# Part of a seven-tap convolution moved from VectorE to GpSimd, and VectorE's calls in another order

## The chip, the cores and the metric

The kernel runs on one core of a Trainium2 chip. The core has TensorE (PE in the profile; its weight loads are PEld), VectorE (DVE), ScalarE (ACT), GpSimd (POOL) and SyncE (SP, which here only issues DMAs). Each engine works through its own list of instructions in order, and the engines wait for one another with semaphores. The metric is the device time of one execution in microseconds (us), as the median of several runs; less is better.

## The reference

The input x has 8 sequences of 4096 tokens with 192 channels. A causal convolution with seven taps runs along the tokens; its weights are a softmax over the taps, one set for each of 8 heads of 24 channels. Its result goes through a feed-forward layer with the exact GELU. The output has 32768 rows of 192.

```python
w = softmax(weight)                                   # 8 heads x 7 taps
x_pad = concatenate([zeros(B, 6, D), x], axis=1)
conv = einsum('hk,bskhg->bshg', w, unfold(x_pad, 7))  # (32768, 192)
h = conv @ w_in                                       # (32768, 2048)
g = 0.5 * h * (1 + erf(h / sqrt(2)))
out = g @ w_out                                       # (32768, 192)
```

## The kernel before

**Tiling.** The tokens are cut into two halves, and both halves are worked side by side: partitions 0 to 63 hold channels of one half, partitions 64 to 127 those of the other. A *block* n takes w tokens from each half, 256 in blocks 0 to 5 and 512 in blocks 6 to 34, so there are 35 blocks. The 192 channels are three *parts* of 64.

**Stages of a block.** SP loads x into one of three buffers `xin`. VectorE transposes it into `xT` (function `trans`, called t below; two buffers). GpSimd copies the last six tokens of the block before into the front of `xT` (`halo`). Then the taps: tap k multiplies a shifted `xT` by a weight for each partition and adds it to `acc` (two buffers). From block 9 on ScalarE makes the first tap, k=0, in three instructions of one part each (`first_tap`). VectorE makes taps 1 to 6 (`conv`, called c1 to c6 below), each one instruction over 1536 elements a partition; c6 writes the bf16 tile `xc`. TensorE makes the first product in 16 *slots* (`mm1`): slot i is 12 matmuls into one of two PSUM buffers `hp`, and ScalarE applies GELU to it and writes it to `gT`. Slot i+2 needs the GELU of slot i, as its buffer is the same. After the 12 matmuls of each slot TensorE makes a share of the second product of the block before (block n-1), in groups of four matmuls, *rounds* below.

**Two kinds of blocks.** Odd blocks from 9 to 33 (the list `ST`, type "S") make their second product by a scheme with fewer matmuls, 44 rounds and not 48. It needs sums of GELU results: VectorE makes `S1`, `S3`, `Dn` and `S4` in pieces (`st_add`; "S1_0" is the first piece of S1), two DMAs from GpSimd's queue with an addition make more (`st_dma`), and the pieces of the result are put together afterwards: ScalarE copies parts out of PSUM (`st_copy`: p5, p1, e, u, p3, -u, -g) and VectorE adds them (`st_post`: k0, k3, k4). All other blocks are type "N". VectorE transposes every block's result from PSUM or SBUF into `osb` (`evac_t`, `st_evac`, three pieces ev0 to ev2), and SP stores it. PSUM's four 512-wide banks of `ob` go from one block's second product to the next; `release` names the instruction that frees a bank.

**The order of the work.** It is written out by hand. TensorE works on block n while VectorE convolves block n+1 or n+2. VectorE's list is a sequence of *loops*, one for the convolution of each block. `plan` has a loop's own calls: t of the next block and then c1 to c6. `AT_ST` and `at_ev` place the other calls: (2, 1, 0, "S1", 0) means the loop of the block's number plus 2, ahead of that loop's call 1. ScalarE's list has 16 GELUs for each block, and `AT_COPY` and `TAPS` say ahead of which slot's GELU a copy or a first tap goes. `ROUNDS` says how many rounds of a type S block's second product follow each slot. GpSimd's list has, for each n, `halo(n)` and then the DMAs of block n-2. SP's list alternates `load(n+4)` and `store(n-1)`.

In the steady state an even block on TensorE carries the second product of a type S block, and an odd block that of a type N block.

Of the kernel before, what the change touches and what calls it, by code (L numbers as in the profile page):

```python
# [11 lines left out]
def bass_lightweight_conv__then__act_gelu_exact_kernel(  # L12
# [16 lines left out]
    TB = 512  # L29
# [42 lines left out]
    ST = [m for m in range(M0 + 3, M1) if m % 2 == 1]  # L72
    K0 = {n: i for i, n in enumerate([4, 5, 6, *range(9, NB)])}
# [48 lines left out]
    with es:  # L122
# [61 lines left out]
        S_K0 = sem("S_K0")  # L184
        S_WT = sem("S_WT")
# [55 lines left out]
        def wait_pc(e, n, p):  # L241
# [11 lines left out]
            n: [(0, 0, 2), (0, 2, 1)] * (n not in K0) + [(k, 0, NP) for k in range(1, KS)]  # L253
            for n in range(NB)
            if n not in PC
        }
        FQ = F // 8
# [55 lines left out]
        def wait_banks(t, m, g):  # L313
# [5 lines left out]
            elif g % 2:  # L319
                t.wait_ge(S_GELU, SL0[NB] - 1 + g // 2)  # L320
            else:
                for b in LAST[g : g + 2]:
                    t.wait_ge(*release(OWNER[b], b))
# [96 lines left out]
        for e, (at, hf, cg, u, k) in enumerate(EVENTS):  # L420
            FIRST.setdefault((UNIT[u][0], cg), e)
        DONE.discard(len(EVENTS) - 1)
        DONE = sorted(DONE)
        ROUNDS = (3, 3, 2, 3, 3, 2, 3, 3, 2, 4, 3, 3, 2, 3, 3, 2)
        assert sum(ROUNDS) == 44

        def st_done(e, m, name):
# [5 lines left out]
        COPIES = ("p5", "p1", "e", "u", "p3", "-u", "-g")  # L433
        AT_COPY = {
            "p5": (1, 6), "p1": (1, 8), "e": (1, 14), "u": (2, 0), "p3": (2, 2), "-u": (2, 6), "-g": (2, 10),
        }

        def ac(m, name):

            return len(COPIES) * ST.index(m) + COPIES.index(name) + 1  # L440

        POSTS = ("k0", "k3", "k4")

        def dp(m, name):

            return len(POSTS) * ST.index(m) + POSTS.index(name) + 1

        SUMS = {"S1": (0, 4, 6, 8), "S3": (6, 8), "Dn": (0, 4, 8), "S4": (0, 4, 8)}

        def sa(m, name, k):  # L450
# [3 lines left out]
        AT_ST = [  # L454
            (2, 1, 0, "S1", 0), (2, 1, 2, "Dn", 0), (2, 1, 4, "S4", 0), (2, 1, 6, "S1", 1),
            (2, 2, 2, "S1", 2), (2, 2, 4, "S3", 0), (2, 3, 0, "Dn", 1), (2, 4, 0, "S4", 1),
            (2, 5, 0, "k0", 0), (3, 1, 0, "ev", 2),
            (3, 6, 0, "k3", 0), (4, 1, 1, "ev", 1), (4, 1, 5, "k4", 0), (4, 2, 0, "ev", 0),
        ]

        def at_ev(n):

            if n == M0:
                return [(3, 1, 3), (3, 2, 1), (3, 2, 3)]
            return [(3, 1, 3), (3, 2, 1), (3, 2, 3)]
# [3 lines left out]
        for n in range(M0, M1):  # L469
            if n not in ST:  # L470
                SIDE += [((n + at[0], *at[1:]), "ev", n, j) for j, at in enumerate(at_ev(n))]
            else:
                SIDE += [((n + d, o, r), name, n, q) for d, o, r, name, q in AT_ST]
        SIDE.sort(key=lambda q: q[0])
        EV = {}
        for _, name, n, j in SIDE:
            if name in ("ev", "evac"):
                EV[n, j] = EVC[M0 - 1] + len(EV) + 1

# [833 lines left out]
```

## Time and profile before

| What | Value |
|---|---|
| median of 3 runs | 669.4 us (668.56 to 669.79) |
| profiled execution, its own time | 667.87 us |
| its span, first to last instruction | 666.1 us |
| granted TensorE clock | 1.00 |
| busy: TensorE, ScalarE, VectorE, GpSimd | 661.4, 610.8, 600.7, 47.6 us |
| GELU: 510 instructions, mean | 1022 ns |
| a tap of 1536 elements on VectorE: mean | 1811 ns |
| t (transposition of a 512 token block): mean | 2369 ns |
| first tap, one part on ScalarE: mean | 718 ns |

The busy time of an engine is what its instructions cover; the ends of TensorE's matmuls are modelled, so its busy share alone doesn't say that it runs at its peak. The profile's parts used below are: the busy table, the chain of work that ended last, the busy times in chosen windows, and the timeline of one engine, whose lines have the start, the length, the engine, the line of the kernel, the tiles and, in brackets, the idle time before and what ended it.

### The profile page before, as it was taken

Reading aid. Unit: us, or ns where it says so; the run is one execution under the profiler, and the core shown is the slowest. Engines: PE = TensorE matmul, PEld = TensorE weight load, DVE = VectorE, ACT = ScalarE, POOL = GpSimd, SP = SyncE. Lnnn points to the kernel's source line nnn. Section 1 sums busy time; section 2 is a strip of 40 time slices with the busy share of each in tenths; the row PEclk is TensorE's granted clock in tenths of the full one; section 3 lists DMA queues with packets and bytes.
Section 4 is the critical chain, followed back from the end, with each engine's and each line's share of the span. In section 5 each row is a group of like instructions: output and inputs, shape, how many; then the busy total and the mean of one; then the engine's idle time right before and its main releaser. Section 6 shows DMA issues by size and latency. Waiting matters only on the chain.

```text
span 666.1 us, 27567 instructions
## 1 busy us (share of the span) xinstructions
PE 661.4 (99%) x12712; PEld 516.4 (78%) x12712; DVE 600.7 (90%) x510; ACT 610.8 (92%) x720; POOL 47.6 (7%) x87
## 2 busy tenths in 40 slices
PE   8999999999999999999999999999999999999998
PEld 8999655557667787877878778787787878878787
DVE  6979999799999999999999999999999999999632
ACT  8999988889999999999999999999999999999884
POOL 7000000010000100001010010100001000010100
PEclk9999999999999999999999999999999999999999
DMA  9735334243081461905529073370824719151233
GB/s 159 165 89 130 65 69 97 72 93 79 18 197 29 107 135 34 203 7 127 114 41 201 3 163 78 62 179 2 191 50 91 151 29 192 22 118 29 56 90 97
DMA packets 137028, 63.92 MB, mean 96 GB/s; under 512 B 126800, under 2 KB 133520, under 8 KB 136912
## 3 DMA queue, kind: packets, MB, share of 16 engines
q1 hardware_dynamic: 129136, 49.37, 33.2%
q0 software_dynamic: 6656, 12.19, 10.1%
q8 instruction: 100, 1.64, 1.1%
q10 hardware_dynamic: 1120, 0.59, 0.3%
q14 instruction: 16, 0.13, 0.1%
HBM read 28.31 MB, written 25.17 MB: 80 GB/s over the span
## 4 chain that ended last, share of the span: by engine, by line
PE 99%; ACT 0%; DVE 0%; DMA 0%; issue 0%; ACTq 0%
PE hp L1066 50%; PE ob L1150 23%; PE ob L1202 18%; PE ob L1106 5%; PE ob L1258 1%; PE hp L1258 1%; PE ob L1011 0%; DMA wsb<-in_weight_dram 0%; PE ob L1066 0%; ACT dg L912 0%; DVE wcol L772 0%; ACT xc L237 0%; ACT osb L347 0%; ACT wex L899 0%; ACT xTb L269 0%
## 5 line engine op out<-in xcount | busy, mean ns | idle before, releaser
L974 ACT ACTIVATE gT<-hp 128x1024 bf16<-128x1024 f32 x510 | 513.0, 1022 | 43.0 <-PE hp L1066 35.7
L1066 PE MATMUL hp<-xc,win 64*64 64x512 bf16 (+2 forms) x6036 | 438.4, 366 | 0.2
L1066 PEld LDWEIGHTS hp<-xc,win 64*64 64x64 bf16 (+1 forms) x6036 | 247.2, 106 | 73.0 <-ACT gT L974 4.6
L827 DVE SCALAR_TENSOR_TENSOR acc<-xT,wcol,acc 128x1536 f32<-128x1536 f32 (+1 forms) x165 | 282.9, 1714 | 10.6 <-ACT acc L938 7.3
L1150 PE MATMUL ob<-gT,wot 64*64 64x512 bf16 x2880 | 205.6, 376 | 0.0
L1202 PE MATMUL ob<-gT,wot 64*64 64x512 bf16 x832 | 158.0, 376 | 0.0
L1150 PEld LDWEIGHTS ob<-gT,wot 64*64 64x64 bf16 x2880 | 112.1, 107 | 43.3
L1202 PE MATMUL ob<-gT,wst 64*64 64x512 bf16 (+2 forms) x832 | 144.0, 323 | 0.0
L1202 PE MATMUL ob<-s_S,wot 64*64 64x128 bf16 (+2 forms) x624 | 89.9, 305 | 0.0
L800 DVE STREAM_TRANSPOSE xT<-xin 128x1536 f32<-128x1536 f32 (+2 forms) x39 | 76.2, 1963 | 3.8 <-DMA xin<-in_x_dram 1.4
L1202 PEld LDWEIGHTS ob<-gT,wst 64*64 64x64 bf16 x832 | 68.5, 107 | 10.7
L1202 PEld LDWEIGHTS ob<-gT,wot 64*64 64x64 bf16 x832 | 63.9, 107 | 1.5
L938 ACT ACTIVATE acc<-xT,wcol 128x512 f32<-128x512 f32 (+1 forms) x87 | 61.2, 703 | 0.0
L827 DVE SCALAR_TENSOR_TENSOR xc<-xT,wcol,acc 128x1536 bf16<-128x1536 f32 (+1 forms) x33 | 56.7, 1720 | 0.8
L1202 PE MATMUL ob<-s_S,wst 64*64 64x512 bf16 x208 | 57.4, 376 | 0.0
L1202 PE MATMUL ob<-s_Dn,wst 64*64 64x512 bf16 x208 | 57.4, 376 | 0.0
L1202 PEld LDWEIGHTS ob<-s_S,wot 64*64 64x64 bf16 x624 | 50.2, 107 | 8.6
L545 POOL DMA_DIRECT2D gT<-gT x26 | 22.4, 861 | 318.1 <-DVE s_S L559 318.1
L1106 PE MATMUL ob<-wout,gT 64*128 64x192 bf16 x768 | 41.9, 243 | 0.0
L1106 PEld LDWEIGHTS ob<-wout,gT 64*128 64x128 bf16 x768 | 35.1, 94 | 3.3
L373 DVE STREAM_TRANSPOSE osb<-ob 128x512 f32<-128x512 f32 x45 | 31.1, 694 | 6.2 <-PE ob L1150 6.2
L559 DVE TENSOR_TENSOR s_S<-gT 128x1024 bf16<-128x1024 bf16 (+1 forms) x39 | 32.6, 837 | 1.4 <-ACT gT L974 1.3
(78 smaller groups left out, 322.6 us busy)
## 6 DMA issues: line engine op xcount, KB each, us to landing
out_dram<-osb SPq DMA_DIRECT2D x124, 192.0 KB, 3.6
xin<-in_x_dram SPq DMA_DIRECT2D x116, 192.0 KB, 4.2
gT<-gT POOLq DMA_DIRECT2D x13, 512.0 KB, 4.6
gT<-gT POOLq DMA_DIRECT2D x13, 256.0 KB, 3.3
xin<-in_x_dram SPq DMA_DIRECT2D x18, 96.0 KB, 2.5
wout<-in_moe_w_out_dram POOLq DMA_DIRECT2D x4, 192.0 KB, 4.7
win<-in_moe_w_in_dram POOLq DMA_DIRECT2D x4, 96.0 KB, 4.3
win<-in_moe_w_in_dram POOLq DMA_DIRECT2D x2, 192.0 KB, 4.5
```

What stands on the lines that cost most here:

```text
L373: v.transpose(osb_t(m, j), bank(BK[m][j])).then_inc(S_EV)
L545: e.dma_start(quad(m, 1, 0, k, k1 - k), quad(m, 0, 0, k, k1 - k), accum_op=ALU.add).then_inc(S_AD[q], 16)
L559: ins = v.tensor_tensor(t("S1"), quad(m, 1, 0, k, n), quad(m, 1, 1, k, n), ALU.add)
L800: v.transpose(out, src).then_inc(S_TR)
L827: ins = v.scalar_tensor_tensor(dst, src, wk, a, op0=ALU.mult, op1=ALU.add)
L938: a.activation(out=acc[n % 2][:, p * TB : p * TB + w], in_=ap(xT[n % 2], p * XW + HX, [[NP * XW, 128], [1, w]]), func=AF.Copy, scale=wcol[ ...
L974: a.activation(out=ap(gT[n % 2], (i % 2 * NF + i // 2) * TB if n in ST else i * c * 2 * w, dst), in_=ap(ob, 2 * TB, [[4 * TB, 128], *src[1 ...
L1066: ins = t.matmul(hbuf(u, slice(fo, fo + fw), o, w), ap(win, f1, [[NP * F, 64], [2, fw]]), xc[n % 2][r, p * TB : p * TB + w], start=(p == 0 ...
L1106: ins = t.matmul(bb[sub], gT[m % 2][r, c0 : c0 + 128], wout[r, CH[sub][i] * C : (CH[sub][i] + 1) * C], start=(ph == 0 and k == 0), stop=(p ...
L1150: ins = t.matmul(bank(BK[m][j], slice(64 * h, 64 * h + 64), w), ap(wot, 64 * hf * NF * C + CH[h][i] * C + 64 * j, [[NF * C, 64], [1, 64]]) ...
L1202: ins = t.matmul(bank(BK[m][bk], slice(64 * cg, 64 * cg + 64))[:, c0 : c0 + w], wt_, x, start=(e == mine[0]), stop=(e == mine[-1] or e in ...
L1258: ins = t.matmul(banks(m, g)[h], gT[m % 2][:, c0 : c0 + 128], wout[:, CH[h][i] * C : (CH[h][i] + 1) * C], start=(i == 0), stop=(i == NF - 1),)
```

## The change

The change does four things.

1. From block 11 on (block 10 keeps seven whole taps) one tap of each block is split. VectorE makes only part 2 of it (512 elements). GpSimd makes parts 0 and 1 in two instructions (`tap_g`): the product of `xT` and the weight is written into the block's `xin` buffer, which the transposition has emptied, and a second instruction adds it to `acc`. In odd blocks this is tap 2, in even blocks tap 4 (`GT`). GpSimd waits for VectorE's tap before it; VectorE's next tap waits for GpSimd's addition (`S_GT`), and so does the load that refills `xin`.
2. VectorE's calls are in another order. In even loops: ev2, c1, c2, k3, c3, k4, ev1, t, S1_0, the third of tap 4 (g), Dn_0, c5, ev0, S1_1, c6. In odd loops: S4_0, ev0 and ev1 of a type N block, S1_2, S3, c1, t, ev2, Dn_1, g, S4_1, k0, c3, c4, c5, c6. Before, t came first in each loop.
3. ScalarE's copies and first taps are ahead of other slots. In an even block: first taps at slots 5, 11, 12 (before 2, 4, 10), p5 at 7 (6), p1 at 9 (8), e at 14 as before. In an odd block: p3 at 1 (2), u at 2 (0), -u at 3 (6), -g at 5 (10), first taps at 8, 10, 13 (4, 8, 12).
4. `ROUNDS` has 4 and 1 rounds after slots 13 and 15 (before 3 and 2). A bank's two halves are freed separately. The tile `tq` has a second buffer, `wtf`. `st_add` has a wait that only two type S blocks in a row would use; there are none here.

TensorE's matmuls are the same in number and shape.

```diff
+    TYPE = {m: "S" if m in ST else "N" for m in range(-4, NB + 4)}
+    LOOPS = {'NNS': 't123456', 'NSN': '1tg3456', 'NSS': '1tg3456', 'SNS': '123tg56', 'SSN': '1tg3456'}
+    FIRST_AT = {'NSN': (5, 11, 12), 'NSS': (4, 8, 12), 'SNS': (8, 10, 13), 'SSN': (12,)}
...
+    ORDER = {n: LOOPS.get(kind(n), "t123456") if n > M0 + 3 else "t123456" for n in range(M0 + 3, NB)}
+    GT = {n: next(k for k in range(1, KS) if str(k) not in o) for n, o in ORDER.items() if "g" in o}
+    PG = 2
...
+        def tap_g(e, n):
+
+            w, kt = WS[n], KS - 1 - GT[n]
+            src = ap(xT[n % 2], HF + kt, [[NP * XW, 128], [XW, PG], [1, w]])
+            z = ap(xin[n % NX], 0, [[TB // 32 * DQ, 128], [TB, PG], [1, w]])
+            a = ap(acc[n % 2], 0, [[NP * TB, 128], [TB, PG], [1, w]])
+            e.tensor_scalar(z, src, wcol[:, kt : kt + 1], None, ALU.mult).then_inc(S_GT)
+            e.wait_ge(S_GT, 2 * list(GT).index(n) + 1)
+            e.tensor_tensor(a, a, z, ALU.add).then_inc(S_GT)
...
-        ROUNDS = (3, 3, 2, 3, 3, 2, 3, 3, 2, 4, 3, 3, 2, 3, 3, 2)
+        ROUNDS = (3, 3, 2, 3, 3, 2, 3, 3, 2, 4, 3, 3, 2, 4, 3, 1)
...
-        AT_COPY = {
-            "p5": (1, 6), "p1": (1, 8), "e": (1, 14), "u": (2, 0), "p3": (2, 2), "-u": (2, 6), "-g": (2, 10),
-        }
+        AT_COPY = {'NN': {'p5': (1, 7), 'p1': (1, 9), 'e': (1, 14), 'p3': (2, 1), 'u': (2, 2), '-u': (2, 3), '-g': (2, 5)}}
...
-        AT_ST = [
-            (2, 1, 0, "S1", 0), (2, 1, 2, "Dn", 0), (2, 1, 4, "S4", 0), (2, 1, 6, "S1", 1),
-            (2, 2, 2, "S1", 2), (2, 2, 4, "S3", 0), (2, 3, 0, "Dn", 1), (2, 4, 0, "S4", 1),
-            (2, 5, 0, "k0", 0), (3, 1, 0, "ev", 2),
-            (3, 6, 0, "k3", 0), (4, 1, 1, "ev", 1), (4, 1, 5, "k4", 0), (4, 2, 0, "ev", 0),
-        ]
+        AT_ST = {'NN': [(1, 4, 10, 'S1', 0),
+                (1, 5, 9, 'Dn', 0),
+                (1, 6, 12, 'S1', 1),
+                (2, 0, 3, 'S1', 2),
+                (2, 0, 6, 'S3', 0),
+                (2, 0, -3, 'S4', 0),
+                (2, 2, 8, 'Dn', 1),
+                (2, 3, 6, 'S4', 1),
+                (2, 3, 7, 'k0', 0),
+                (3, 0, 5, 'ev', 2),
+                (3, 2, 4, 'k3', 0),
+                (3, 3, 9, 'ev', 1),
+                (3, 3, -3, 'k4', 0),
+                (3, 6, 1, 'ev', 0)]}
+        AT_EV = {'NS': [(3, 0, -2), (3, 0, 3), (3, 2, -3)], 'SS': [(3, 0, -2), (3, 0, 3), (3, 2, -3)]}
...
+            if n - NX in GT:
+                e.wait_ge(S_GT, 2 * list(GT).index(n - NX) + 2)
...
-            for n in range(3, M1 + 2):
+            for n in range(3, M1 + 3):
                 if n < NB:
                     halo(n)
+                if n - 1 in GT:
+                    g.wait_ge(S_HALO, n)
+                    g.wait_ge(S_CV, cvd(n - 2) + [q[0] for q in CALLS[n - 1]].index(GT[n - 1]))
+                    tap_g(g, n - 1)
...
+                if n in GT and k == GT[n] + 1:
+                    v.wait_ge(S_GT, 2 * list(GT).index(n) + 2)
```

## The prediction

> **What bounds the kernel now.** I read the page's busy table and the chain of work that ended last first.
>
> ```profile
> PE 661.4 (99%) x12712; PEld 516.4 (78%) x12712; DVE 600.7 (90%) x510; ACT 610.8 (92%) x720; POOL 47.6 (7%) x87
> ...
> PE 99%; ACT 0%; DVE 0%; DMA 0%; issue 0%; ACTq 0%
> ```
>
> TensorE is the chain from end to end. Since its matmul ends are modelled, that alone doesn't show that it runs at its peak, so I asked for the busy times of single pairs of blocks (one odd, one even), among them the last, where VectorE has far less to do.
>
> ```profile
> 278.88:319.48 40.60, 40.60 (x791) 32.66 (x786) 39.20 (x32) 38.45 (x46) 2.46 (x4) 1.00 0.47 98
> 563.12:603.73 40.61, 40.61 (x794) 32.66 (x787) 39.18 (x32) 38.46 (x46) 2.55 (x4) 1.00 0.40 87
> 603.73:644.34 40.61, 40.61 (x793) 32.79 (x787) 28.22 (x26) 36.08 (x41) 1.71 (x2) 1.00 0.28 61
> ```
>
> The columns after the stretch and its length are the busy times of PE, PEld, DVE, ACT and POOL. VectorE falls from 39.2 to 28.2 us and the pair still takes 40.61: TensorE sets the pace, and VectorE's freed time buys nothing. Next, TensorE's own timeline, in which any late operand would show as an uneven step.
>
> ```profile
> 246.25 0.87 PE L1066 MATMUL hp<-xc,win 64*64 64x512 bf16 x12
> 246.90 0.87 PE L1150 MATMUL ob<-gT,wot 64*64 64x512 bf16 x12
> ...
> 276.90 0.41 PEld L1066 LDWEIGHTS hp<-xc,win 64*64 64x64 bf16 x12 [0.21 <-ACT gT L974]
> ...
> 276.91 0.89 PE L1066 MATMUL hp<-xc,win 64*64 64x512 bf16 x12
> ```
>
> Twelve matmuls take 0.65 us, so a round of four takes 0.216, and a slot with three rounds 1.295. The steps are even to a few hundredths. The one place where ScalarE nearly delays TensorE is slot 8 of an even block (last two lines): the GELU of slot 6 ends at 276.84, the weight loads start 0.05 later, the matmuls just in time; that block loses 0.02 us. So the question is not what VectorE gains, but which engine now comes late for TensorE. ScalarE is the nearest.
>
> ```profile
> 247.50 2.00 ACT L974 ACTIVATE gT<-hp 128x1024 bf16<-128x1024 f32 x2
> 249.52 0.59 ACT L598 ACTIVATE tq<-ob 64x512 f32<-64x512 f32 x1
> 250.14 1.95 ACT L974 ACTIVATE gT<-hp 128x1024 bf16<-128x1024 f32 x2
> 251.99 0.71 ACT L938 ACTIVATE acc<-xT,wcol 128x512 f32<-128x512 f32 x1
> 252.60 1.01 ACT L974 ACTIVATE gT<-hp 128x1024 bf16<-128x1024 f32 x1
> 253.87 1.02 ACT L974 ACTIVATE gT<-hp 128x1024 bf16<-128x1024 f32 x1 [0.26 <-PE hp L1066]
> 254.92 0.63 ACT L598 ACTIVATE uu<-uu 64x512 f32<-64x512 f32 x1
> 255.57 1.94 ACT L974 ACTIVATE gT<-hp 128x1024 bf16<-128x1024 f32 x2
> ```
>
> From start to start: GELU to GELU 0.92; GELU to a first tap (L938) 0.92, and 0.61 from there to the next GELU; to p3 (or p5) 1.05 and 0.62; to -u (or -g) 1.05 and 0.65; to u (or p1) 0.92 and 0.48. A slot is 1.295, so a GELU with a copy (1.56 to 1.70) runs 0.3 to 0.4 late and the next slot gives 0.37 back. Before, the extras stand at least two slots apart. A GELU can start 0.92 after its slot's first matmul (253.87 against 252.95 for slot 5).
>
> **The change, part by part.** Times in an odd block count from its first matmul (246.25 above).
>
> *VectorE's work.* 24 taps (blocks 11 to 34) shrink from 1536 to 512 elements. The profile has 1.81 us for 1536 and 1.02 for 768, so 512 take about 0.75: 24 x 1.06 = 25 us less busy, worth 0 by the windows above; only ScalarE's schedule and the new waits are left.
>
> *ScalarE's copies in odd blocks.* p3, u, -u stand at slots 1, 2, 3, -g at 5. GELU 0 starts at 0.97 (kept back by that of the slot before), p3 2.02, GELU 1 2.64, u 3.56, GELU 2 4.04, -u 5.08, GELU 3 5.74, which ends at 6.76. Slot 5 is due at 4 x 1.295 + 0.65 + 4 x 0.216 = 6.69 and can start about 0.08 after that end: **0.15 us lost**. Then GELU 4 6.66, -g 7.71, GELU 5 8.36, ending 9.38; slot 7, due at 9.28 + 0.15, loses 0.03. Together 0.18 in each of 12 odd blocks (11 to 33): 2.2 us. If p3, -u and -g cost only 0.92 ahead of them, this is 0; if starts slip by 0.1, 0.3.
>
> *The first tap at slot 8 and t.* Odd block o's slot 8 makes the first tap of block o+2, which needs t of that block; t now stands behind k3, c3, k4 and ev1 in VectorE's list. k3 waits for -u and k4 for -g.
>
> ```profile
> 255.58 0.69 DVE L608 TENSOR_TENSOR tq<-tq,uu 128x512 f32<-128x512 f32 x1 [0.96 <-ACT uu L598]
> 256.19 1.81 DVE L827 SCALAR_TENSOR_TENSOR xc<-xT,wcol,acc 128x1536 bf16<-128x1536 f32 x1
> 258.09 2.41 DVE L800 STREAM_TRANSPOSE xT<-xin 128x1536 f32<-128x1536 f32 x1
> ```
>
> These lines show the links: k3 0.03 after -u ends, the next call 0.61 later, a tap 1.81, t 2.40. -u ends at 5.71: k3 5.74, c3 6.35 to 8.16, k4 after -g (8.34) at 8.37, ev1 8.97, t 9.60 to 12.00. The tap would start at 11.3 and starts at 12.06 (0.06, as GpSimd's copy follows VectorE below), GELU 8 at 12.67, ending 13.69. Slot 10, due at 10 x 1.295 + 2 x 0.216 (two slots have four rounds) + 0.18 = 13.56, can start at 13.77: **0.21 lost** in 11 odd blocks (11 to 31): 2.3 us. This is one to one in t's end: at 11.8 it is 0, at 12.3 0.5.
>
> *Even blocks.* Slots with 3, 3, 2 rounds: GELU 4 5.89, first tap 6.81, GELU 5 7.42, GELU 6 8.33, p5 9.38, GELU 7 10.00, ending 11.02; slot 9, due at 9 x 0.65 + 24 x 0.216 = 11.03, loses 0.07, and the 0.02 of slot 8 goes: 0.05 in 13 blocks, 0.65. The first taps at 11 and 12 end with GELU 12 at 17.6, slot 14 due at 17.73. ROUNDS moves one round from slot 15 to slot 13: nothing in the sum.
>
> *GpSimd's pair.* Its product has one input: 256 elements took 0.405, 18 took 0.210, so 1024 about 1.04 (at most 1.10, by the 768-element copy of 0.822). The addition has two: 256 bf16 elements took 0.614. Bounds for 1024: 1.24 with the slope of one input, 2.46 in proportion; I take 1.86, the row's slope over the smallest copy's 0.2. With 0.06 between them: 3.0 (2.3 to 3.6). In the even loop it starts at 8.22, behind c3, and ends at 11.2 (at the latest 11.85), while VectorE runs k4, ev1 and t.
>
> ```profile
> 242.22 0.20 POOL L723 COPY xT<-xT 128x18 f32<-128x18 f32 x1 [14.88 <-DVE xc L827]
> ...
> 267.10 0.96 POOL L723 COPY xT<-xT 128x18 f32<-128x18 f32 x1
> ```
>
> The same copy takes 0.20 next to t and 0.96 when it starts inside a tap (266.20 to 268.00); it ends 0.06 after the tap. So GpSimd waits for a VectorE instruction that reads two SBUF tiles, and the reverse is likely. Next is S1_0, which reads two, at 11.94: no meeting, 0. In the odd loop the pair starts behind c1; t and ev2 cover 2.9 us, and Dn_1 may wait up to 0.75. That loop's c6 ends 1.3 us before TensorE needs `xc`: hidden; without that cover, 12 x 0.75 = 9 us. The next tap, g's successor c3 or c5, comes 3 us or more after the pair.
>
> [...]
>
> *Other moved calls.* ev0 of a type N block frees the bank for the first rounds of an even block: S1_0 11.94, g 13.05, Dn_0 13.7, c5 14.85, ev0 16.6, S1_1 17.2, c6 17.8, S4_0 19.5, that ev0 20.6 to 21.35, needed at 20.72 + 0.39 + 0.65 = 21.76: margin 0.3 with the weight load ahead. Then t ends 6.45 into the even block, its tap is due at 6.8. p5, p1 and k0 come 0.6, 0.8 and 2 us before TensorE reads them. VectorE now idles some 2.7 us a pair at k3. On SP, `load` waits for the pair, and the stores behind it need ev calls of a later loop anyway; x is there over 30 us before t. On POOL, the DMA for S1_0 is queued behind the pair, but S1_0 itself comes later than its end; `halo` waits only for c6. All cost 0.
>
> *Sum.* 2.2 + 2.3 + 0.65 = 5.1 us on the profiled execution's 667.87 (span 666.1, 1.8 around it): 673.0. That execution is 1.5 under the median of 669.4, so I forecast **674.5**.
>
> **The rivals.** *No change.* The three losses are each 0.05 to 0.2 us, against rows known to 0.02 to 0.05; if TensorE starts a little closer behind a GELU and t ends 0.2 sooner, all vanish: 669.4. *k4 counts as a two-input instruction.* It reads PSUM and SBUF; if it waited for GpSimd's product (until 9.3), t and the tap at slot 8 would come 0.95 later: 11 x 0.95 = 10 more, 685. No row has such a pair. *GpSimd is half as fast as taken.* A pair of 5.8 ends at 14.0 and holds S1_0 by 2.1, of which 0.3 is margin: 1.8 x 11 = 20 more, 694. It decides from a pair of 4.1 us on; the rows stop at 3.6. *Faster.* The pitch of a round (0.216 us) would have to shrink because VectorE touches SBUF less: 1% of some 465 us (186 to 652) would be 4.5 us, 665. It counts from 0.3% of the pitch on; the last pair, with VectorE down to 28 us and the same 40.61, speaks against it.
>
> **How the numbers follow.** Forecast (1.5 to 9 us more) 0.60, no change 0.18, k4 0.09, GpSimd slow 0.08, faster 0.05. 0.2% (1.3 us) is about what a measurement tells here. Slower 0.77, the same 0.18, faster 0.05. The range from 669.0 to 685.5 leaves out the fast case, a little of no change and the slow GpSimd.
>
> **What would show it.** Pairs of 41.0 us; idle TensorE or weight loads ended by GELUs at slots 5 and 10 of odd blocks; about 0.7 us of ScalarE's idle time before its first tap, ended by t; k3 waiting some 2.7 us for -u; VectorE 25 us less busy; GpSimd's addition near 1.9 us. Wrong if pairs stay 40.6, or if TensorE waits for VectorE.

## The result, and the profile after

The changed kernel takes 692.76 us (median of its runs, 692.32 to 692.99), against 669.4 before: 1.035 times as long, with a 95% interval of 1.0327 to 1.0374. The profiled execution took 692.32 (span 690.6, against 666.1). The forecast was 674.5 with a range of 669.0 to 685.5: the direction was right, the size was not. The time is that of one of the rivals, the slow GpSimd pair (694).

The page's busy table after, and the first line of the chain of work that ended last:

```profile
PE 675.4 (98%) x12712; PEld 447.2 (65%) x12712; DVE 617.7 (89%) x510; ACT 610.4 (88%) x720; POOL 188.4 (27%) x135
...
DVE 42%; PE 28%; ACT 11%; issue 10%; POOL 9%; DVEq 0%; POOLq 0%
```

Two things stand out. The chain was 99% PE and is now led by DVE, with POOL in it. And DVE, which gives away two thirds of a tap in 24 blocks, is busy for 617.7 us, 17 more than the 600.7 of before. Somewhere its instructions have become longer.

Pairs of blocks (one odd, one even), in the view of busy times by stretch of time; the columns after the stretch and its length are the busy times of PE, PEld, DVE, ACT and POOL:

```profile
251.40:294.07 42.67, 41.72 (x791) 25.89 (x784) 40.58 (x32) 38.39 (x46) 14.10 (x8) 1.00 0.44 95
422.09:464.77 42.68, 41.71 (x790) 26.00 (x784) 40.59 (x32) 38.39 (x46) 14.11 (x8) 1.00 0.43 95
```

Each of these pairs takes 42.67 us instead of 40.60. The first pair with a split tap takes 41.02, the eleven behind it 42.67, so 11 x 2.07 + 0.42 = 23.2 of the span's 24.5 us lie in this stretch. TensorE idles 0.95 in each, which it didn't before. The granted clock is 1.00 in all rows, so the other 1.12 us are no slower clock; as the ends of matmuls are modelled, a late matmul can count as busy, so the losses are read from when the matmuls start (below).

VectorE and GpSimd in one even loop, from the timeline:

```profile
472.64 0.69 DVE L685 TENSOR_TENSOR gsm<-ob,gsm 128x512 f32<-128x512 f32 x1 [0.26 <-ACT gsm L671]
473.25 0.70 DVE L697 STREAM_TRANSPOSE osb<-wtf 128x512 f32<-128x512 f32 x1
473.87 2.36 DVE L877 STREAM_TRANSPOSE xT<-xin 128x1536 f32<-128x1536 f32 x1
476.14 2.80 DVE L626 TENSOR_TENSOR s_S<-gT 128x2048 bf16<-128x2048 bf16 x1
478.86 0.74 DVE L288 SCALAR_TENSOR_TENSOR acc<-xT,wcol,acc 128x512 f32<-128x512 f32 x1
```

```profile
472.55 2.85 POOL L295 TENSOR_SCALAR xin<-xT,wcol 128x1024 f32<-128x1024 f32 x1 [8.22 <-DVE acc L288]
475.49 2.37 POOL L297 TENSOR_TENSOR acc<-acc,xin 128x1024 f32<-128x1024 f32 x1
```

In the kernel before, S1_0's group has a mean of 1185 ns:

```profile
L559 DVE TENSOR_TENSOR s_S<-gT 128x2048 bf16<-128x2048 bf16 x13 | 15.4, 1185 | 1.3 <-ACT gT L974 1.3
```

The product takes 2.85 us and the addition 2.37, so the pair takes 5.30 and ends at 477.86. S1_0 (L626) starts at 476.14, inside the addition, and takes 2.80 where it took 1.19 before. It ends 1.08 after the addition, a little less than its usual length, so it did next to nothing until GpSimd was done. Here an instruction that stands like this is called *held*. Before it, k4 (L685, one input in PSUM and one in SBUF) and the transpositions stand beside the product at their usual lengths (0.69, and 0.70 and 2.36, against means of 0.68, 0.70 and 2.37 in the kernel before).

The odd loop, in the same two views:

```profile
450.89 1.22 DVE L632 TENSOR_TENSOR s_Dn<-gT,s_S 128x2048 bf16<-128x2048 bf16 x1
452.00 2.90 DVE L288 SCALAR_TENSOR_TENSOR acc<-xT,wcol,acc 128x512 f32<-128x512 f32 x1
454.81 1.21 DVE L635 TENSOR_TENSOR s_S<-gT,s_Dn 128x2048 bf16<-128x2048 bf16 x1
```

```profile
448.35 2.84 POOL L295 TENSOR_SCALAR xin<-xT,wcol 128x1024 f32<-128x1024 f32 x1 [4.44 <-DVE acc L288]
451.28 3.06 POOL L297 TENSOR_TENSOR acc<-acc,xin 128x1024 f32<-128x1024 f32 x1
```

Here Dn_1 is at work when the addition comes, and the addition waits (3.06 instead of 2.37). Then VectorE's own third of the tap waits for the addition: 2.90 us for an instruction that takes 0.74 in the even loop. So both directions of the hold are in the trace. A held instruction counts as busy in the profile, and that explains most of DVE's busy time: 13 x (2.73 - 1.19) = 20 us more for S1_0 and 24 x (1.81 - 0.75) = 25 us more for the short taps, by the means of their groups, against 25 us that the shorter taps gave away; the sum is 20, and 17 were measured.

What TensorE waits for, and in one line ScalarE, from the view of the waits (idle us, how often, the longest):

```profile
PEld hp L1136 <- ACT gT L1044: 30.8, 72, 0.7
PEld ob L1273 <- DVE osb L416: 13.0, 12, 1.1
...
ACT acc L1009 <- DVE xT L877: 7.7, 11, 0.7
...
PE ob L1273 <- DVE osb L416: 7.2, 12, 0.6
...
PE hp L1136 <- DVE xc L288: 3.2, 12, 0.3
```

L416 is the transposition that frees a bank (ev0 of a type N block), and L1273 the second product of a type S block: TensorE stands ahead of slot 1 of the even blocks. In the kernel before no such wait is listed. The first line, 4.6 us in the kernel before, is weight loads that wait for a GELU; some 14 us of it fall at slot 0, where `xc` ends after that GELU, and the rest at slots 5, 7 and 10 of odd blocks and slot 9 of even ones.

For a table place by place, the distance from each slot's first product (the 12 matmuls, by the start of the last one) to that of the slot before is compared with the same distance in the kernel before: means over blocks 15 to 31, the moved round taken out, good to some 0.02 us. These are the losses of one pair of blocks in the changed kernel and in the eleven variants below, in us:

| kernel | median, ratio (95%) | pair | odd 0 (xc) | odd 5, 7 | odd 10 | even 0 (xc) | even 1 (ev0) | even 7 to 10 |
|---|---|---|---|---|---|---|---|---|
| before | 669.4 | 40.60 | | | | | | |
| changed | 692.76, 1.035 (1.033-1.037) | 42.67 | 0.47 | 0.04 | 0.21 | 0.24 | 1.01 | 0.09 |
| whole_tap | 679.61, 1.0166 (1.0144-1.0187) | 41.60 | 0 | 0.13 | 0.14 | 0 | 0.73 | 0 |
| one_part | 674.01, 1.0076 (1.0054-1.0098) | 41.10 | 0 | 0.12 | 0.18 | 0 | 0.19 | 0 |
| idle_pair | 706.89, 1.0571 (1.0545-1.0597) | 43.87 | 0.47 | 0.04 | 0.19 | 0.85 | 1.01 | 0.69 |
| cheap_product | 675.41, 1.0107 (1.0090-1.0124) | 41.22 | 0.08 | 0.05 | 0.18 | 0 | 0.32 | 0 |
| memsets | 672.54, 1.0060 (1.0045-1.0075) | 40.93 | 0 | 0.13 | 0.20 | 0 | 0 | 0 |
| late_first_tap | 673.64, 1.0078 (1.0063-1.0093) | 41.09 | 0 | 0.13 | 0 | 0 | 0.37 | 0 |
| less_vectore | 668.61, 0.9999 (0.9989-1.0008) | 40.60 | 0 | 0 | 0 | 0 | 0 | 0 |
| ev0_sooner | 692.19, 1.0344 (1.0326-1.0363) | 42.7 | 0.47 | 0.05 | 0.20 | 0.25 | 0 | 1.13 |
| pair_ahead | 686.35, 1.0262 (1.0241-1.0284) | 42.16 | 0.47 | 0.05 | 0 | 0 | 0.93 | 0.09 |
| pair_ahead_cheap | 674.49, 1.0080 (1.0064-1.0097) | 41.16 | 0.07 | 0.06 | 0 | 0 | 0.42 | 0 |
| no_meeting | 674.25, 1.0086 (1.0072-1.0100) | 41.15 | 0 | 0.12 | 0 | 0 | 0.42 | 0 |

The ratios compare with runs of the kernel before on the same chip, whose medians were 668.49 to 669.01. A twelfth variant, "sizes", was run for its durations only.

### The profile page after: what moved, and what is told of

It reads as the page before. It is cut to its first block, busy times and chain, and to the rows that moved or that the text cites. A ratio compares the mean times of both kernels' runs of the same rounds, so it can differ in the third digit from the quotient of the medians.

```text
span 690.6 us, 27697 instructions
## 1 busy us (share of the span) xinstructions
PE 675.4 (98%) x12712; PEld 447.2 (65%) x12712; DVE 617.7 (89%) x510; ACT 610.4 (88%) x720; POOL 188.4 (27%) x135
## 4 chain that ended last, share of the span: by engine, by line
DVE 42%; PE 28%; ACT 11%; issue 10%; POOL 9%; DVEq 0%; POOLq 0%
PE hp L1136 14%; DVE acc L288 13%; ACT gT L1044 8%; DVE s_S L626 7%; DVE xc L288 6%; PE ob L1176 5%; POOL acc L297 4%; PE ob L1221 4%; DVE s_S L635 4%; POOL xin L295 4%; DVE xT L877 4%; DVE s_Dn L632 2%; PE ob L1273 2%; DVE osb L416 2%; ACT uu L671 2%
## 5 line engine op out<-in xcount | busy, mean ns | idle before, releaser
L1136 PE MATMUL hp<-xc,win 64*64 64x512 bf16 (+2 forms) x6036 | 449.3, 367 | 4.0 <-DVE xc L288 3.2
L1136 PEld LDWEIGHTS hp<-xc,win 64*64 64x64 bf16 (+1 forms) x6036 | 217.9, 105 | 123.4 <-ACT gT L1044 30.8
L288 DVE SCALAR_TENSOR_TENSOR acc<-xT,wcol,acc 128x1536 f32<-128x1536 f32 (+2 forms) x165 | 283.0, 1715 | 9.3 <-ACT acc L1009 6.5
L1221 PE MATMUL ob<-gT,wot 64*64 64x512 bf16 x2880 | 196.6, 376 | 0.0
L1273 PE MATMUL ob<-gT,wot 64*64 64x512 bf16 x832 | 176.1, 377 | 7.2 <-DVE osb L416 7.2
L1273 PE MATMUL ob<-gT,wst 64*64 64x512 bf16 (+2 forms) x832 | 149.0, 323 | 0.0
L1221 PEld LDWEIGHTS ob<-gT,wot 64*64 64x64 bf16 x2880 | 83.5, 107 | 72.0 <-DVE osb L697 3.5
L295 POOL TENSOR_SCALAR xin<-xT,wcol 128x1024 f32<-128x1024 f32 x24 | 68.2, 2843 | 161.1 <-DVE acc L288 161.1
L1273 PEld LDWEIGHTS ob<-gT,wot 64*64 64x64 bf16 x832 | 71.5, 107 | 33.0 <-DVE osb L416 13.0
L1273 PE MATMUL ob<-s_S,wot 64*64 64x512 bf16 (+2 forms) x624 | 92.0, 306 | 0.0
L1273 PEld LDWEIGHTS ob<-gT,wst 64*64 64x64 bf16 x832 | 69.2, 107 | 3.2
L796 POOL COPY xT<-xT 128x18 f32<-128x18 f32 x30 | 18.7, 622 | 179.2 <-DVE xc L288 138.4
L297 POOL TENSOR_TENSOR acc<-acc,xin 128x1024 f32<-128x1024 f32 x24 | 65.3, 2719 | 2.1
L1273 PE MATMUL ob<-s_S,wst 64*64 64x512 bf16 x208 | 59.6, 377 | 0.0
L626 DVE TENSOR_TENSOR s_S<-gT 128x1024 bf16<-128x1024 bf16 (+1 forms) x39 | 52.2, 1339 | 7.1 <-ACT gT L1044 7.1
L1273 PE MATMUL ob<-s_Dn,wst 64*64 64x512 bf16 x208 | 57.4, 376 | 0.0
L1273 PEld LDWEIGHTS ob<-s_S,wot 64*64 64x64 bf16 x624 | 49.4, 106 | 2.7
```

The costliest lines, as they stand in the source:

```text
L288: return e.scalar_tensor_tensor(dst, src, wk, a, op0=ALU.mult, op1=ALU.add)
L295: e.tensor_scalar(z, src, wcol[:, kt : kt + 1], None, ALU.mult).then_inc(S_GT)
L297: e.tensor_tensor(a, a, z, ALU.add).then_inc(S_GT)
L626: ins = v.tensor_tensor(t("S1"), quad(m, 1, 0, k, n), quad(m, 1, 1, k, n), ALU.add)
L1136: ins = t.matmul(hbuf(u, slice(fo, fo + fw), o, w), ap(win, f1, [[NP * F, 64], [2, fw]]), xc[n % 2][r, p * TB : p * TB + w], start=(p == 0 ...
L1221: ins = t.matmul(bank(BK[m][j], slice(64 * h, 64 * h + 64), w), ap(wot, 64 * hf * NF * C + CH[h][i] * C + 64 * j, [[NF * C, 64], [1, 64]]) ...
```

## The experiments

**What GpSimd's instructions cost alone (sizes).** The kernel before, with ten GpSimd instructions at its end, one after the other, when nothing else runs.

```diff
...
+            g.wait_ge(S_MM2, MMC[NB])
...
+            tests = [
+                lambda: g.tensor_scalar(zt(0, 2), xs(2), wk, None, ALU.mult),
+                lambda: g.tensor_scalar(zt(0, 1), xs(1), wk, None, ALU.mult),
+                lambda: g.tensor_scalar(zt(0, 2), xs(2), 0.5, None, ALU.mult),
+                lambda: g.tensor_copy(zt(0, 2), xs(2)),
+                lambda: g.tensor_tensor(zt(1, 2), at(2), zt(0, 2), ALU.add),
...
+                lambda: g.tensor_tensor(zt(1, 2), xs(2), ap(wcol, 4, [[32, 128], [0, 2], [0, TB]]), ALU.mult),
...
```

> The kernel before, with ten GpSimd instructions behind its last DMA, once TensorE has ended and VectorE has little left: the product and the addition of the change and forms near them, one after the other. In the changed kernel the product of 1024 elements takes 2.84 us and the addition 2.37 where nothing holds it. Theory one: the product is that slow by itself, and alone takes 2.84 again, and half of it with 512 elements (1.4). Rival: the transposition t, which ran beside every one of the 24 products, holds it up; alone it takes 1.0 to 1.1, as the prediction had it. The addition alone: 2.4 by both. A copy of 1024 elements: near 1.1 if the slow product is a matter of the multiplication, near 2.8 if it is one of float32 reading.

GpSimd's groups of the profile (the last figure ahead of the second bar is the mean in ns):

```profile
L762 POOL TENSOR_SCALAR xin<-xT,wcol 128x1024 f32<-128x1024 f32 x1 | 2.9, 2851 | 33.1 <-PE hp L1286 33.1
...
L764 POOL TENSOR_SCALAR xin<-xT 128x1024 f32<-128x1024 f32 x1 | 2.8, 2768 | 0.1
L766 POOL TENSOR_TENSOR xin<-acc,xin 128x1024 f32<-128x1024 f32 x1 | 2.3, 2338 | 0.1
L768 POOL TENSOR_TENSOR xin<-xT,wcol 128x1024 f32<-128x1024 f32 x1 | 1.9, 1892 | 0.1
L763 POOL TENSOR_SCALAR xin<-xT,wcol 128x512 f32<-128x512 f32 x1 | 1.6, 1556 | 0.1
...
L765 POOL COPY xin<-xT 128x1024 f32<-128x1024 f32 x1 | 1.0, 1036 | 0.1
```

The product takes 2.85 us alone, so the 2.84 in the kernel is its own length and not a wait for VectorE's t. It is not the reading and writing: a copy of the same size takes 1.04. The scalar from a column (2.85) or as a constant (2.77) makes little difference. The same product as a two-input multiplication by the column laid out with a step of zero takes only 1.89. The addition takes 2.34. (This run's own time contains the ten instructions and says nothing of the change.)

**No GpSimd at all (whole_tap).** The changed kernel, but VectorE makes the whole tap in the place of "g".

```diff
-    GT = {n: next(k for k in range(1, KS) if str(k) not in o) for n, o in ORDER.items() if "g" in o}
+    GS = {n: next(k for k in range(1, KS) if str(k) not in o) for n, o in ORDER.items() if "g" in o}
+    ORDER = {n: o.replace("g", str(GS.get(n))) for n, o in ORDER.items()}
+    GT = {}
```

> The change without GpSimd's part: VectorE makes the whole tap, in the new order and with ScalarE's new slots. Theory one (GpSimd's pair of 5.3 us holds S1_0 in even loops and g in odd loops): S1_0 takes 1.2 and not 2.8, g 1.8 in both loops; the chain from -u to the first ev0 of the odd loop falls from 17.2 to 16.7 us, the odd loop by 1.1, a pair of blocks takes 41.6 and not 42.7, the time is 682. Rival, that the new order alone makes the loss and GpSimd adds nothing: 693 or more, since VectorE has 25 us more to do.

679.61, pairs of 41.60: without any split the kernel is 13 us faster than the changed one. The new order of VectorE's and ScalarE's calls costs 1.7% by itself, with whole taps. Of the 1.0 us per pair 0.27 are ScalarE's slots, and 0.73 are slot 1 of even blocks, where ev0 is late even with no hold.

**One part on GpSimd (one_part).** `PG = 1`, so that GpSimd makes 512 elements and VectorE 1024.

> The change with GpSimd making one part of the tap and not two: 512 elements, VectorE 1024. Theory one: the pair is about 2.7 us, ends ahead of S1_0, which takes 1.2 again; what is left is g's extra 0.5 us and the losses behind ScalarE at slots 7, 9 and 10; a pair of blocks takes 41.1, the time is 675 to 677. Rival, that the waits for GpSimd or the GpSimd instructions themselves cost, whatever their length: 690.

674.01, a little under the 675 to 677 expected, and pairs of 41.10. The product takes 1.56 and the addition 1.31; S1_0 is at 1.24; Dn_1, which now meets the end of the addition in odd loops, is held for some 0.2 (the group of Dn_0 and Dn_1 has a mean of 1.33, against 1.21 in the changed kernel). That is faster than without GpSimd, so in the new order a short split does give something: slot 1 of even blocks loses 0.19 instead of 0.73.

**The pair without the wait (idle_pair).** VectorE makes the whole taps, and GpSimd runs the same two instructions at the same place on its own buffer. No tap waits for them.

```diff
...
-            e.tensor_tensor(a, a, z, ALU.add).then_inc(S_GT)
+            e.tensor_tensor(z, z, z, ALU.add).then_inc(S_GT)
...
-                if n in GT and k == GT[n] + 1:
-                    v.wait_ge(S_GT, 2 * list(GT).index(n) + 2)
```

> As the kernel in which VectorE makes the whole tap, but GpSimd runs its two instructions of 1024 elements at the same places all the same; its addition goes from its own buffer to its own buffer, and no tap waits for it. If what costs is that VectorE's instructions with two SBUF inputs can't run beside GpSimd's (the lock), S1_0 takes 2.8 and g in the odd loop is held until the addition ends, now with 1.8 us of its own behind it: a pair of blocks near 45, the time 700 to 720. If what costs is the tap's wait for the addition, this is as fast as the kernel with the whole tap (682).

706.89, inside the 700 to 720 expected, with pairs of 43.87 where 45 were expected. The groups of VectorE that meet the pair, and the pair itself:

```profile
L289 DVE SCALAR_TENSOR_TENSOR acc<-xT,wcol,acc 128x1536 f32<-128x1536 f32 x145 | 282.4, 1948 | 5.7 <-ACT acc L1010 3.5
L627 DVE TENSOR_TENSOR s_S<-gT 128x2048 bf16<-128x2048 bf16 x13 | 29.8, 2293 | 6.1 <-ACT gT L1045 6.1
```

```profile
L296 POOL TENSOR_SCALAR xin<-xT,wcol 128x1024 f32<-128x1024 f32 x24 | 68.2, 2843 | 162.2 <-DVE acc L289 162.2
...
L298 POOL TENSOR_TENSOR xin<-xin 128x1024 f32<-128x1024 f32 x24 | 54.0, 2249 | 2.1
```

Against whole_tap, which lacks GpSimd's two instructions, the pair costs 27 us though no tap waits for its result (only a transposition two blocks later waits for the product, so that its buffer isn't overwritten). So the loss is not the new wait but the hold: VectorE's instructions with two inputs in SBUF stand while GpSimd's addition works (S1_0 takes 2.29 instead of 1.20, and the taps 1.95 on average instead of 1.82).

**The same length without reads (memsets).** The product and the addition are replaced by five fills of the same buffer. Two thirds of one tap per block are left out.

```diff
-            e.tensor_scalar(z, src, wcol[:, kt : kt + 1], None, ALU.mult).then_inc(S_GT)
-            e.wait_ge(S_GT, 2 * list(GT).index(n) + 1)
-            e.tensor_tensor(a, a, z, ALU.add).then_inc(S_GT)
+            for j in range(5):
+                e.memset(z, 0.0).then_inc(S_GT)
+                e.wait_ge(S_GT, 5 * list(GT).index(n) + j + 1)
...
```

> The changed kernel, with GpSimd's product and addition replaced by five fills of the same x buffer (0.95 us each alone, one after the other; two thirds of one tap per block are left out). The time that GpSimd is busy, its place and the waits on it are kept (about 5.2 us against 5.30); what is gone is that it reads SBUF with one or two inputs. If the hold by the pair's reading costs the time: S1_0 is back at about 1.2 us, g no longer takes 2.9, the pairs of blocks fall to 41.2 to 41.7 and the time to 675 to 682. If the wait of the next tap for a 5.3 us long pair costs it: pairs of 42.7 and 690 to 694.

672.54, a little under the range expected if reading is what holds. Timeline of the even loop, first VectorE and then GpSimd:

```profile
463.86 1.25 DVE L626 TENSOR_TENSOR s_S<-gT 128x2048 bf16<-128x2048 bf16 x1
464.95 0.82 DVE L288 SCALAR_TENSOR_TENSOR acc<-xT,wcol,acc 128x512 f32<-128x512 f32 x1
```

```profile
460.23 4.99 POOL L296 MEMSET xin<- 128x1024 f32 x5 [9.62 <-DVE acc L288]
```

GpSimd is busy from 460.23 to 465.22, through S1_0 and the short tap, and they take 1.25 and 0.82. GpSimd's length, its place and the wait on it are nearly as in the changed kernel, the reads are gone, and with them 20 of the 23 us. S1_0, with two inputs in SBUF, took 2.80 beside the addition, which reads SBUF, and takes 1.25 beside the fills, which only write it. Where Dn_1 was at work first, the addition took 3.06 and not 2.37. Not every GpSimd instruction that reads SBUF holds VectorE, though: the multiplication by a scalar reads it too, and the short tap took 0.71 inside it (shown under cheap_product).

What is left in this run is ScalarE's part alone: 0.10 at slot 5, 0.03 at slot 7 and 0.20 at slot 10 of odd blocks.

**A cheaper product (cheap_product).** The two-input form from the first experiment.

```diff
-            e.tensor_scalar(z, src, wcol[:, kt : kt + 1], None, ALU.mult).then_inc(S_GT)
+            wk = ap(wcol, kt, [[32, 128], [0, PG], [0, w]])
+            e.tensor_tensor(z, src, wk, ALU.mult).then_inc(S_GT)
```

> The changed kernel, with the product written as a two-input multiplication by the column laid out with a step of zero (1.89 us alone for 1024 elements) in place of the multiplication by a scalar operand (2.85). Theory one (GpSimd's length sets the time, through the hold on S1_0 in even loops and on Dn_1 in odd ones): the pair is 1.89 + 0.09 + 2.37 = 4.35 us against 5.30, ends 0.95 earlier, S1_0 lasts about 1.9 instead of 2.80, and the first second-product round of even blocks loses under 0.3 instead of 1.01: pairs of blocks 41.5 to 42.0, time 679 to 686. Theory two (GpSimd's length decides nothing; the other order of VectorE's calls costs it): 692, as changed. [...]

675.41, pairs of 41.22: better than either theory had it, and 17 us faster than the changed kernel by one instruction's form. In the even loop:

```profile
465.65 1.85 DVE L627 TENSOR_TENSOR s_S<-gT 128x2048 bf16<-128x2048 bf16 x1
467.42 0.74 DVE L288 SCALAR_TENSOR_TENSOR acc<-xT,wcol,acc 128x512 f32<-128x512 f32 x1
```

S1_0 takes 1.85, as expected from a pair that is 0.95 shorter; the loss at slot 1 of even blocks falls to 0.32. What I had left out is that the same 0.95 also helps in the odd loop: VectorE's third of the tap is no longer held (its group has a mean of 753 ns, against 1811), though Dn_1 now is (the group of Dn_0 and Dn_1 has a mean of 1.96, against 1.21). The waits for `xc` at slot 0, 0.71 us of the changed kernel's 2.07, are nearly gone.

The two forms of the product also differ in what they hold. In the steady loops the product meets no VectorE call with two inputs in SBUF but the start of Dn_1. In the last loop, which has no t, VectorE's third of the tap falls into the middle of it. First the changed kernel, then cheap_product, from the timelines of GpSimd and VectorE:

```profile
643.31 2.84 POOL L295 TENSOR_SCALAR xin<-xT,wcol 128x1024 f32<-128x1024 f32 x1 [18.21 <-DVE acc L288]
644.63 0.71 DVE L288 SCALAR_TENSOR_TENSOR acc<-xT,wcol,acc 128x512 f32<-128x512 f32 x1
...
626.93 1.90 POOL L296 TENSOR_TENSOR xin<-xT,wcol 128x1024 f32<-128x1024 f32 x1 [19.39 <-DVE acc L288]
628.29 1.09 DVE L288 SCALAR_TENSOR_TENSOR acc<-xT,wcol,acc 128x512 f32<-128x512 f32 x1
```

Inside the multiplication by a scalar the tap takes its usual length and ends 0.81 before it. Inside the two-input product it takes 1.09 and ends 0.55 after it: held. Dn_1, which starts 0.28 before the end of the changed kernel's odd products, takes its usual 1.21. So the changed kernel's product holds neither of the two calls that meet it: its 2.85 us cost time by moving the addition, which does hold, onto S1_0 and the odd loop's tap. The two-input form does hold the short tap (1.09 instead of 0.74), but it is shorter, and in the steady loops no VectorE call with two inputs in SBUF falls into it.

**A later first tap (late_first_tap).** One part on GpSimd, with the first taps of odd blocks at slots 9, 11 and 13.

```diff
-    FIRST_AT = {'NSN': (5, 11, 12), 'NSS': (4, 8, 12), 'SNS': (8, 10, 13), 'SSN': (12,)}
+    FIRST_AT = {'NSN': (5, 11, 12), 'NSS': (4, 8, 12), 'SNS': (9, 11, 13), 'SSN': (12,)}
...
-    PG = 2
+    PG = 1
```

> One part of three on GpSimd (674.0 us, pairs of 41.10), with the first taps of blocks after an odd block at slots 9, 11 and 13 instead of 8, 10 and 13. The prediction's step for slot 10: a tap and another ScalarE instruction before the GELU of slot 10 lose 0.21 per odd block. If this is right, that loss goes (11 times 0.21, some 2.3 us) and slots 9 and 11 lose no more than 0.05: pairs of 40.85 to 40.95, time 671 to 672.5. If only the place of the loss moves: pairs of 41.1 and 674.

Slot 10 of odd blocks does lose nothing now, which confirms the cause of its 0.2 us. But pairs are 41.09 and the time 673.64, as in one_part: slot 1 of even blocks lost 0.19 and now loses 0.37. What TensorE wins ahead of a late ev0, it gives back by waiting for it. The first half of the expectation held, and the second (671 to 672.5) didn't.

**Relief alone (less_vectore).** The kernel before, in which VectorE makes tap 2 for one part of three only. Two thirds of that tap are left out.

```diff
-            n: [(0, 0, 2), (0, 2, 1)] * (n not in K0) + [(k, 0, NP) for k in range(1, KS)]
+            n: [(0, 0, 2), (0, 2, 1)] * (n not in K0) + [(k, 0, NP) if k != 2 or n < 11 else (k, 2, 1) for k in range(1, KS)]
```

> The kernel before, unchanged but for tap 2 of every block from 11 on, which VectorE makes for one part of three only (two thirds of one tap are left out; nothing is put on GpSimd). VectorE is relieved of the same work that the change moves, about 25 us. The prediction's first step gives this nothing, as TensorE is the bound: pairs of blocks 40.6, time 668.5 to 669.5. If VectorE's time were worth something in the kernel before: 660 to 667.

```profile
246.69:287.29 40.60, 40.60 (x789) 32.65 (x785) 37.06 (x32) 38.45 (x46) 2.46 (x4) 1.00 0.48 100
571.77:612.36 40.59, 40.59 (x789) 33.52 (x785) 36.25 (x33) 38.44 (x46) 2.35 (x3) 1.00 0.27 61
```

VectorE is busy 575.4 us instead of 600.7, and the ratio is 0.9999 (0.9989 to 1.0008). In the old order the 25 us that the change takes from VectorE are worth nothing, even if GpSimd did its part for free.

**Another place for ev0 (ev0_sooner).** The changed kernel with ev0 of type N blocks ahead of S4_0.

```diff
-        AT_EV = {'NS': [(3, 0, -2), (3, 0, 3), (3, 2, -3)], 'SS': [(3, 0, -2), (3, 0, 3), (3, 2, -3)]}
+        AT_EV = {'NS': [(3, 0, -2), (3, 0, 3), (3, 2, -3)], 'SS': [(3, 0, -4), (3, 0, 3), (3, 2, -3)]}
```

> The changed kernel, with the first transposition of a type N block's result (ev0, which frees the bank that TensorE waits for in slot 1 of even blocks) put ahead of S4_0 instead of behind it in VectorE's list: ev0 comes 1.14 us sooner, S4_0 0.7 later. If only ev0's place makes the hold on S1_0 costly, slot 1 of even blocks no longer loses 1.01 us and the pairs of blocks fall from 42.67 to 41.6 to 41.8: 680 to 683. If VectorE's whole list from k3 (which waits for -u) to xc is what TensorE now waits for, the loss moves to another slot, above all to the wait for xc at slot 0 of odd or even blocks: pairs of 42.4 to 42.7 and 688 to 693.

692.19, and pairs of 42.7: slot 1 of even blocks loses nothing, slots 7 to 10 lose 1.13 instead of 0.09. The second alternative holds, though not at the place it named. ev0 is only the first thing that TensorE sees of a late VectorE. Whatever stands behind the held call in VectorE's list is late, and one of them is waited for.

**The pair beside other calls (pair_ahead and pair_ahead_cheap).** The even loops in the order of the odd ones, so that S1_0 comes after the tap that waits for the pair. The second run also has the cheap product.

```diff
-    LOOPS = {'NNS': 't123456', 'NSN': '1tg3456', 'NSS': '1tg3456', 'SNS': '123tg56', 'SSN': '1tg3456'}
+    LOOPS = {'NNS': 't123456', 'NSN': '1tg3456', 'NSS': '1tg3456', 'SNS': '1tg3456', 'SSN': '1tg3456'}
```

> The changed kernel, with the even loops in the order 1tg3456 that the odd loops have, instead of 123tg56. GpSimd's pair then runs beside t, k3, k4 and ev1 of the even loop, and S1_0 comes behind the tap that waits for the pair, so it can't be held by it; the lengths of the product and of the addition stay as they are, and so does the odd loop. Theory one (the hold on S1_0 is the even loop's loss): S1_0 is back at about 1.2 us, slots 0, 1 and 10 of even blocks lose nothing, t comes early enough for the first tap at slot 8, so slot 10 of odd blocks loses at most 0.1; what stays is slot 5 (0.1 to 0.15) and at most 0.47 at slot 0 of odd blocks: pairs of 40.75 to 41.3, time 671 to 677. If it is the length of the pair and the wait behind it wherever it stands: pairs of 42 and more, 684 to 693.

> The same order 1tg3456 in even loops, with the product written as a two-input multiplication by the column with a step of zero (1.89 us instead of 2.85). If the odd loop's hold on Dn_1 and g is what is left over in the run before, the shorter pair takes most of it away: pairs of 40.7 to 40.9, time 670 to 672.5. None of the two theories has a time below 668.5, since TensorE's own pace is 40.60 a pair.

pair_ahead takes 686.35, the number that the second theory had, but not for its reason. Timeline of VectorE and then of GpSimd in the even loop:

```profile
462.75 2.35 DVE L877 STREAM_TRANSPOSE xT<-xin 128x1536 f32<-128x1536 f32 x1
466.18 2.67 DVE L681 TENSOR_TENSOR wtf<-wtf,uu 128x512 f32<-128x512 f32 x1 [1.08 <-ACT uu L671]
...
472.35 1.21 DVE L626 TENSOR_TENSOR s_S<-gT 128x2048 bf16<-128x2048 bf16 x1
```

```profile
463.00 2.85 POOL L295 TENSOR_SCALAR xin<-xT,wcol 128x1024 f32<-128x1024 f32 x1 [2.45 <-DVE acc L288]
465.94 2.36 POOL L297 TENSOR_TENSOR acc<-acc,xin 128x1024 f32<-128x1024 f32 x1
```

S1_0 is back at 1.21, as expected, but the hold has moved to k3 (L681), which also reads two SBUF tiles and takes 2.67 instead of 0.69. I had counted k3 among the calls that hide the pair. It ends 0.55 after the addition. With t early, slot 10 of odd blocks loses nothing. With the cheap product the time is 674.49, pairs of 41.16; the odd loop's wait falls from 0.47 to 0.07, as expected, but slot 1 of even blocks keeps 0.42, so that it missed the expected 670 to 672.5.

**A pair that meets nothing (no_meeting).** One part, cheap product, the order 1tg3456 everywhere.

> One part of three on GpSimd, the product as a two-input multiplication by the column, the order 1tg3456 in all loops: the pair is 1.0 + 0.1 + 1.3 = 2.4 us, so that it ends beside t in both kinds of loop, and no call of VectorE that reads two SBUF tiles meets it. Theory one (holds alone, beyond ScalarE's slots, cost TensorE time): no instruction of VectorE is longer than in the kernel before; slot 5 of odd blocks keeps its 0.10, slot 1 of even blocks loses less than the 0.42 of the run with two parts: pairs of 40.75 to 41.0, time 670 to 673. If VectorE's list in the new order is too long also without a hold (as it was with whole taps, where slot 1 lost 0.73): 0.73 less some 0.5 for the shorter tap, 0.2 at slot 1: pairs of 40.9 to 41.1, 672 to 674. In neither case is it faster than the kernel before.

674.25, pairs of 41.15. The pair takes 1.04 + 0.08 + 1.28 = 2.40 us and lies beside t; S1_0 takes 1.23 and k3 0.69. So no hold is left, and of the two alternatives the second is nearer, that VectorE's list in this order is too long by itself; but slot 1 of even blocks loses 0.42 and not the 0.2 it had, as much as in pair_ahead_cheap, where k3 was held (1.69). VectorE's timeline shows why it is the same number:

```profile
458.99 0.69 DVE L682 TENSOR_TENSOR wtf<-wtf,uu 128x512 f32<-128x512 f32 x1 [2.19 <-ACT uu L672]
459.59 1.28 DVE L288 SCALAR_TENSOR_TENSOR acc<-xT,wcol,acc 128x1024 f32<-128x1024 f32 x1
461.67 0.69 DVE L686 TENSOR_TENSOR gsm<-ob,gsm 128x512 f32<-128x512 f32 x1 [0.80 <-ACT gsm L672]
...
473.28 1.22 DVE L636 TENSOR_TENSOR s_S<-gT,s_Dn 128x2048 bf16<-128x2048 bf16 x1
474.42 1.31 DVE L417 STREAM_TRANSPOSE osb<-ob 128x512 f32<-128x512 f32 x2
```

k4 (L686) waits 0.80 us for ScalarE's -g copy at slot 5 (0.34 in pair_ahead_cheap). From there to ev0 (the first of the two transpositions at 474.42) VectorE runs without a gap, 12.75 us of calls that are the same in both runs (there from 462.20 to 474.95). This chain, slot 5 of an odd block to slot 1 of the next even one, is too long by 0.42. That follows from the two traces; a kernel with -g at another slot was not tried.

No variant beats the kernel before, and the run with less work on VectorE says why no relief of VectorE alone can: with 25 us less to do on VectorE and no GpSimd, TensorE's pair still takes 40.60.

## Why the prediction was wrong

**What was right.** *VectorE's work*, worth 0: less_vectore shows 0.9999. *ScalarE's copies in odd blocks*, 0.15 + 0.03: 0.10 and 0.03 where VectorE is not late (memsets). In the changed kernel these two show only 0.04, since TensorE already stands 0.47 at the start of the block. *The first tap at slot 8 and t*, 0.21: 0.21 at slot 10, ScalarE idle 7.7 us in 11 odd blocks (0.7 each) ended by t. Moving that tap takes it away. *Even blocks*, 0.05: nothing measurable net. These steps together are worth 3.8 us in memsets, against the 5.1 of the sum; memsets' 672.54 is about the kernel that I had forecast, one whose pair holds no one. The k4 rival is refuted: beside the product k4 takes 0.69, and so it does beside the two-input product of cheap_product, which held a call with two inputs in SBUF (the short tap, 1.09 instead of 0.74). *Dn_1 may wait up to 0.75*: it took 1.22, no longer than usual, and the addition waited for it (3.06 instead of 2.37).

**The step that failed: *GpSimd's pair*.** It took the product for "about 1.04 (at most 1.10)", with the slope of a copy with one input, and it takes 2.85. A copy of 1024 elements does take 1.04; multiplying by a scalar takes 1.8 us more, and no row of the profile had such a multiplication. The addition was taken at 1.86 (up to 2.46) and measured 2.37, inside its range (2.34 alone). So the pair is 5.30 instead of 3.0, the addition began where the whole pair should have ended, its end came at 13.5 us after the odd block's first product and not at 11.2, and "no meeting, 0" became a meeting of 1.7 us with S1_0, which started at 11.8 (forecast 11.94). In the odd loop the same length met VectorE's third of the tap, a call that the step didn't count as one that could be held; the prediction looked at Dn_1 alone. A second premise of the step was half right: it took from the copy that GpSimd's reading and VectorE's two-input calls exclude each other, and of the pair only the addition held VectorE (S1_0 took 2.80 beside it, the short tap 0.71 beside the product).

**What carried it to TensorE.** The prediction had the mechanism and the price in its rival: a late S1_0 pushes ev0, of which 0.3 us is margin, 1.8 per pair. It measured 2.07 less ScalarE's 0.25, 1.8. The margin was about right: with whole taps, 1.06 us longer than the short ones, ev0 costs 0.73 (whole_tap), and with taps longer by 0.53 it costs 0.19 (one_part), so some 0.33 is hidden. That the totals agree is partly luck: S1_0 is held by 1.6 and not by 2.1, the loss is 1.01 at ev0, 0.71 at the two waits for `xc` and 0.1 later, and 0.47 of it, the wait ahead of odd blocks, comes from the odd loop, which the rival didn't have (with the odd loop unchanged, pair_ahead still has the 0.47). Its bound of 4.1 us for the pair was of the right kind: at 4.35 (cheap_product) the loss beyond ScalarE's slots is 0.4. It had 0.08 of the chances because "the rows stop at 3.6". That was the mistake in judging: the upper end of the product came from copies, and no row had a multiplication with one input.

**What would have shown it.** Pairs were 42.67 and not 41.0; k3 waited 1.7 us for -u on average (12.7 and 9.0 us over 13) and not 2.7, since VectorE was later; VectorE was not 25 us less busy but 17 more; the addition was 2.37 or 3.06 and not near 1.9. "Wrong if TensorE waits for VectorE" was the right test: it waits for it at slot 0 and slot 1.

## What to carry to other kernels

The work put on GpSimd beside a busy VectorE had two prices here: its length (5.30 us), and the wait of the VectorE calls with two inputs in SBUF that fell into its addition (2.80 us instead of 1.19 for S1_0, 2.90 instead of 0.74 for the short tap, 2.67 instead of 0.69 for k3), also where no tap needed the result (27 us in idle_pair). For such a move, list those calls for the longest plausible length, in all kinds of loops. An operation whose kind has no row in the profile should be bounded by the slowest operation of like size that the engine shows, not by a copy: here that is 2.46 us (0.614 for 256 elements, in proportion), which is still short of 2.85 but makes a pair of 5.0, past the 4.1 at which the rival decides. And work taken off an engine that the bound doesn't wait for is worth nothing by itself (0.9999 here), so any reordering that goes with it starts with a loss.

## What was unexpected of the hardware

GpSimd's multiplication by a scalar was the slower of two ways to multiply: 2.85 us for 1024 float32 elements a partition (1.56 for 512), against 1.89 (1.04 for 512, in no_meeting) as a two-input multiplication by a column with a step of zero, and 1.04 for a copy of 1024.

The slower form was the one that let VectorE work: calls with two inputs in SBUF took 0.71 us (the short tap) and 1.21 (Dn_1, of which 0.28 lay beside it), their usual lengths, and the short tap 1.09 instead of 0.74 beside the two-input product. The addition held them nearly completely: three different calls (S1_0, the short tap, k3) ended 1.08, 0.56 and 0.55 us after it, a little less than their own lengths of 1.19, 0.75 and 0.69, so they did next to nothing while they stood.
